# Part of a key sum moved from an accumulator to one-column matmuls, two tiles projected from centred rows, and all engine orders made anew

## Chip, cores, metric

One core of one Trainium2 chip. The metric is device time in microseconds (us), the median over several executions. All runs quoted are of the fast state (a single run is called so); the granted clock in the records is 0.996 to 1.0. Executions of one and the same kernel spread over 0.9 us and more, so an effect of a few tenths is read from traces, not from times.

## The reference, cut

Two layers of linear attention and two gated feed-forward layers, in turn, on a sequence of 2048 rows and width 512 (16 tiles of 128 rows):

```python
phi = lambda t: jnp.where(t > 0, t + 1, jnp.exp(t)) + 1e-6
pq, pk = phi(q), phi(k)                          # q, k, v = layernorm(x) @ wqkv, 32 heads of 16
kv  = jnp.einsum("bhsd,bhse->bhde", pk, v)
z   = jnp.einsum("bhsd->bhd", pk)                # sum of the keys over all rows
num = jnp.einsum("bhqd,bhde->bhqe", pq, kv)
den = jnp.einsum("bhqd,bhd->bhq", pq, z)[..., None] + 1e-6
x = x + (num / den) @ wo                         # layers 0 and 2
x = x + (silu(h @ w_gate) * (h @ w_up)) @ w_down # layers 1 and 3, h = layernorm(x)
```

## The kernel before

Every operation is put on one of five engines in an order that is written out. `PROGRAM` is PE's order; its tokens are a layer digit, a letter and a number. `k4` is the projection of key tile 4, `q23` of the queries of rows group 2, column block 3, `g` the state product pk^T x (four accumulators, 16 tiles), `z` a one-column sum of one tile on PE, `s` the two halves of a sum made elsewhere, `d` denominators, `v`, `m`, `r`, `w` the rest of attention, `u` gate and up, `n` down, `t` a transpose on PE, `S` a spin that keeps PE's clock up. `ORDER` holds the orders of the other engines (`.ts` and `.phi` are DVE's two steps of phi, `.exp` and `.id1` ACT's, `.sq` a sum of squares, `.vpe` variance plus epsilon, `.zs` an addition to the key sum, `.pqn` the scaling of queries by the transposed reciprocal, `.evac` a copy out of an accumulator). `ON_ACT` names what runs on ACT, or on DVE instead of POOL.

```python
def phi(pb, dst, dk, name):
    e = r_e.take()
    on_act = name in ON_ACT
    op("act", lambda a: a.activation(out=etmp[e][:], in_=PB[pb][:], func=ACT.Exp), ...)          # .exp
    if on_act:
        op("act", lambda a: a.activation(out=dst, in_=PB[pb][:], func=ACT.Identity, bias=onep[:]), ...)  # .id1
    op("dve", ... etmp = min(etmp, 1) + 1e-6 ...)                                                # .ts
    if on_act: op("dve", ... dst = max(dst, etmp) ...)               # .phi, two inputs in SBUF
    else:      op("dve", ... dst = max(PB[pb] + 1 + 1e-6, etmp) ...) # .phi, one input in PSUM

def z_add(L, t):                       # layer 2: all 16 tiles, into a float tile zs
    eng = "dve" if f"{L}b{t}" in ON_ACT else "pool"
    op(eng, lambda v: v.tensor_tensor(out=zs, in0=zs, in1=pk[t][:], op=ALU.add), ...)   # .zs

def z_sum(L):                          # token 2s
    op("dve", ... hi = bf16(zs) ...)   # .zh
    op("dve", ... lo = zs - hi ...)    # .zl
    for i, src in enumerate((hi, lo)): # 8 one-column matmuls
        for c in range(NC): mm(pb, src[:, c*P:(c+1)*P], ones[:], ...)
    z_fin(L, pb)                       # mask, on DVE: Zm
# ... cut: layer 0 has a token 0z<t> for each tile (z_acc), 4 one-column matmuls each
# PROGRAM, layer 2:
# 2q20 2q22 2k13 2q23 2g2 2k12 2g7 2g6 2g14 2q13 2s 2d01 2g12 2d02 2g1
# DVE at 49 us:  0q22.phi 0q23.ts 0d0.pqn2 0q23.phi 0G1.evac
```

Of the kernel before, what the change touches and what calls it, by code (L numbers as in the profile page):

```python
# [164 lines left out]

PROGRAM = """
S S S S S S S S S S S S S S S S S S S S S S S S S S S S S S S S S S S S S S S S S S 0t0 S S S S S S S S 0k0 S S S S
0t1 S S S 0t2 S S S 0k1 0k2 S 0t3 0g0 0g1 0k3 0g2 0k4 0k5 0g3 0k10 0g4 0k9 0g5 0k6 0k7 0q03 0z0 0g10 0z4 0k8 0k15
0g7 0k13 0k12 0g9 0k11 0z2 0z10 0z9 0q11 0z3 0z5 0z8 0z15 0g6 0z13 0k14 0q02 0z7 0q10 0q01 0q00 0z1 0g11 0q12 0q21
0z14 0z12 0z6 0z11 0q13 0d02 0d03 0d01 0d00 0g8 0q20 0d11 0q22 0g13 0d12 0d13 0d10 0q23 0d20 0g15 0g12 0g14 0d23  # L170
0d22 0d21 0q30 0v 0q31 0m0 0m1 0m2 0m3 0r2 0w3 0w2 0q33 0w1 0w0 0w5 0w11 0q32 0w7 0w6 0w9 0d33 0w8 0w4 0w10 1u011
1u007 1u005 1u008 1u002 1u006 0d31 0d32 1u012 1u003 1u013 0d30 1u010 1u004 1u000 1u110 1u001 1u009 1n3 0w14 1n0 0w12
1u106 1n1 1u102 1n2 1u107 1u204 0w13 1u101 0w15 1u111 2k2 1u109 1u105 1u103 1u104 1u108 2k0 1u100 2k1 2q00 1u112
1u113 2k3 1n7 1u209 1n6 1u211 1u205 1n4 1n5 1u213 1u200 1u303 1u202 1u203 2q10 1u301 1u208 1u309 1u304 1u206 1u212
2g0 1u201 1u311 1u302 2q11 1u305 1u207 1u310 2q01 1u308 2q03 1u312 2q02 1u210 1n11 1u313 2k4 1u300 1n8 1n10 1u306
1n9 1u307 2k8 1n14 2k7 2k10 2k5 2q21 1n15 2k6 2k9 2k11 1n13 1n12 2q12 2k15 2k14 2g3 2g5 2q20 2q22 2k13 2q23 2g2 2k12
2g7 2g6 2g14 2q13 2s 2d01 2g12 2d02 2g1 2d00 2d03 2d20 2d13 2d21 2q30 2d22 2d10 2d12 2d11 2g13 2q31 2g10 2d23 2g15
2g4 2g9 2g11 2g8 2r1 2q32 2v 2q33 2m0 2m1 2m2 2m3 2d31 2d30 2w0 2w1 2w2 2d32 2w3 2w6 2w5 2w11 2d33 2w4 2w8 2w7 2w9
2w10 3u008 3u000 3u009 3u013 3u010 3u004 3u003 3u005 3u007 3u103 3u110 3u108 3u012 3u002 3u001 3u006 3u104 2w13
3u011 3n3 3u100 2w12 3n2 3n0 3u106 3u105 2w14 3u107 3u111 3n1 3u102 3u109 3u112 3u101 3u113 3n6 3n4 3n5 3n7 3u200  # L180
3u201 3u202 3u203 3u204 2w15 3u205 3u206 3u207 3u208 3u209 3u210 3u211 3u212 3u213 3n8 3n9 3n10 3n11 3u300 3u301
3u302 3u303 3u304 3u305 3u306 3u308 3u307 3u309 3u310 3u311 3u312 3u313 3n12 3n13 3n14 3n15
# [4 lines left out]
i.ld i.ld1 0x2.stats 0x2.sq 0x7.stats 0k0.exp 0t1.xT 0t2.xT 0x10.stats 0k1.exp 0x10.sq 0k2.exp 0t3.xT 0x15.stats  # L187
0x12.stats 0x7.sq 0k3.exp 0x15.sq 0x12.sq 0k4.exp 0k5.exp 0x13.stats 0x13.sq 0k10.exp 0k10.id1 0k9.exp 0k9.id1
0x14.stats 0x14.sq 0k6.exp 0k7.exp 0k6.id1 0q03.exp 0x11.apply 0k8.id1 0k8.exp 0k15.exp 0k15.id1 0k13.exp 0k12.exp
0k13.id1 i.c 0k11.exp 0q11.id1 i.c1 0q11.exp 0k14.id1 0k14.exp 0q02.exp 0q02.id1 0q10.exp 0q01.id1 0q01.exp 0q00.exp  # L190
i.c3 0q12.id1 0q12.exp i.c2 0q21.exp 0q21.id1 0q13.id1 0q13.exp 0d0.rep 0d0.rep2 0q20.exp 0d0.rep1 0q22.exp 0d0.rep3
0q23.exp 0q23.id1 0d1.rep1 0G0.evac 0G2.evac 0G3.evac 0d1.rep 0q30.id1 0q30.exp 0q31.exp 0q31.id1 0M1.evac 0M3.evac
0d1.rep3 0d1.rep2 1x3.sq 1x2.sq 0q33.id1 1x1.sq 0q33.exp 1x0.sq 0q32.exp 1x5.sq 0q32.id1 1x11.sq 1x7.sq 1u011.tanh
1u007.tanh 1x6.sq 1u005.tanh 1u008.tanh 1u002.tanh 1u006.tanh 1x6.apply 1x9.sq 1u012.tanh 1u003.tanh 1u013.tanh
1x4.sq 1u010.tanh 1u004.tanh 1u000.tanh 1x10.sq 0d3.rep2 1u110.tanh 1u001.tanh 0d3.rep 1u009.tanh 1x8.sq 1x10.apply
1x8.apply 1x14.sq 2x3.sq 0d3.rep1 0d3.rep3 2x1.sq 1u102.tanh 1u106.tanh 1u107.tanh 2x2.sq 1u204.tanh 1u101.tanh
2x0.sq 1x13.sq 2k2.id1 1u111.tanh 2k2.exp 1u109.tanh 1u105.tanh 1u103.tanh 2x1.apply 1u104.tanh 1u108.tanh 1x12.sq
2k0.exp 2k0.id1 2k1.id1 2q00.id1 2k1.exp 1u100.tanh 1u112.tanh 1u113.tanh 2q00.exp 1x15.sq 2k3.id1 2k3.exp 2x7.sq
1u209.tanh 2x6.sq 1u211.tanh 1x13.apply 2x4.sq 1u205.tanh 2x6.apply 1u213.tanh 2x5.sq 2x7.apply 1u200.tanh
1u303.tanh 2x5.apply 1u203.tanh 1u202.tanh 2q10.id1 2q10.exp 1u301.tanh 1u208.tanh 1u309.tanh 1u304.tanh 1u206.tanh  # L200
1u212.tanh 1u201.tanh 1u311.tanh 1u302.tanh 2q11.id1 2q11.exp 1u305.tanh 1u207.tanh 1u310.tanh 2q01.exp 2q01.id1
1u308.tanh 2q03.exp 2q03.id1 1u312.tanh 2q02.exp 2q02.id1 1u210.tanh 1u313.tanh 2k4.exp 1u300.tanh 2x11.sq 2k4.id1
2x8.sq 1u306.tanh 2x10.sq 2x8.apply 1u307.tanh 2x9.sq 2x10.apply 2x9.apply 2k8.id1 2k8.exp 2k7.exp 2x14.sq 2k7.id1
2k10.exp 2q21.id1 2k5.id1 2k5.exp 2q21.exp 2k6.exp 2x14.apply 2k9.exp 2x15.sq 2k11.exp 2k9.id1 2x13.sq 2q12.exp
2k15.exp 2x12.sq 2k15.id1 2k14.exp 2q20.exp 2k13.exp 2q22.exp 2q23.id1 2q22.id1 2k12.exp 2q23.exp 2q13.id1 2q13.exp
2d0.rep 2d0.rep1 2d0.rep2 2q31.exp 2q30.exp 2d0.rep3 2q31.id1 2d2.rep 2G0.evac 2G2.evac 2G3.evac 2q32.id1 2d2.rep1
2q32.exp 2d2.rep2 2M0.evac 2M1.evac 2M2.evac 2q33.exp 2q33.id1 2d2.rep3 3x0.sq 3x2.sq 3x1.sq 3x3.sq 3x6.sq 3x5.sq
3x11.sq 3u008.tanh 3u000.tanh 3u009.tanh 3x7.sq 3u013.tanh 3u010.tanh 3x4.sq 3u004.tanh 3u003.tanh 3u005.tanh
2d3.rep 3u103.tanh 2d3.rep1 3u007.tanh 3x9.sq 3u110.tanh 3x8.sq 3u108.tanh 2d3.rep2 3u002.tanh 3u012.tanh 3u001.tanh
2d3.rep3 3u006.tanh 3u104.tanh 3u011.tanh 3u100.tanh 3x13.sq 3x12.sq 3u106.tanh 3u105.tanh 3u107.tanh 3u111.tanh  # L210
3x10.sq 3x13.apply 3u109.tanh 3x10.apply 3u102.tanh 3u101.tanh 3u113.tanh 3u112.tanh 3u200.tanh 3u201.tanh
3u202.tanh 3u203.tanh 3u205.tanh 3u204.tanh 3u207.tanh 3u206.tanh 3u208.tanh 3u209.tanh 3x15.sq 3x14.sq 3u211.tanh
3u210.tanh 3u212.tanh 3u213.tanh 3u300.tanh 3u301.tanh 3u302.tanh 3u303.tanh 3u304.tanh 3u306.tanh 3u305.tanh
3u307.tanh 3u308.tanh 3u309.tanh 3u310.tanh 3u312.tanh 3u311.tanh 3u313.tanh
""",
    "dve": """
i.c 0x0.stats 0x0.aggr 0x0.vpe 0x1.stats 0x1.aggr 0x0.apply 0x3.stats 0t0.xT 0x4.stats 0x3.aggr 0x4.aggr 0x1.apply
0x2.apply 0x5.stats 0k0.ts 0x4.apply 0x5.aggr 0k0.phi 0x3.apply 0x9.stats 0k1.ts 0k1.phi 0x9.aggr 0k2.ts 0x5.apply
0k2.phi 0x6.stats 0x10.apply 0x6.aggr 0x9.apply 0x8.stats 0k3.ts 0k3.phi 0x7.vpe 0x6.apply 0x8.aggr 0k4.ts 0k4.phi
0x7.apply 0k5.ts 0k5.phi 0x12.vpe 0x8.apply 0k10.ts 0k10.phi 0x11.stats 0x11.aggr 0x15.apply 0x11.vpe 0x13.apply  # L220
0x12.apply 0x14.vpe 0k7.ts 0k6.ts 0k7.phi 0q03.ts 0k9.ts 0k9.phi 0k6.phi 0q03.phi 0x14.apply 0k8.ts 0k12.ts 0k15.ts
0k8.phi 0k15.phi 0k12.phi 0k13.ts 0k11.ts 0k13.phi 0k11.phi 0k14.ts 0q11.ts 0q02.ts 0k14.phi 0q11.phi 0q02.phi
0q10.ts 0q10.phi 0q01.ts 0q01.phi 0q00.ts 0q00.phi 0z.zm 0q12.ts 0d0.den 0d0.den1 0q13.ts 0q12.phi 0q13.phi 0q21.ts
0q21.phi 0q20.ts 0q20.phi 0d1.den 0q22.ts 0d1.den1 0q22.phi 0q23.ts 0d0.pqn2 0q23.phi 0G1.evac 0d0.pqn1 0d2.den
0d2.den1 0d0.pqn3 0v.mask 0q30.ts 0d2.den2 0d1.pqn1 0M0.evac 0M2.evac 0d0.pqn 0r2.pqn 0w3.res 0r2.pqn1 0w2.res
0r2.pqn2 1x3.apply 0r2.pqn3 0w1.res 1x2.apply 0w0.res 0d1.pqn3 0d1.pqn2 0q33.ts 1x1.apply 0q33.phi 0d1.pqn 0w5.res
1x0.apply 0w11.res 0w9.res 1x5.vpe 0w7.res 0w6.res 0q32.ts 1x5.apply 0w4.res 1x11.vpe 0w10.res 1x7.vpe 1u011.gst
0w8.res 1u011.h 0q31.ts 1x11.apply 0q31.phi 0q30.phi 1u007.gst 1u007.h 1x6.vpe 1u005.gst 1u008.gst 1u008.h 1u005.h
0q32.phi 1u006.gst 1u006.h 1u002.gst 1u002.h 1u012.gst 1x7.apply 1u012.h 1u003.gst 1x4.vpe 0d3.den 1x4.apply 1u003.h
1x9.apply 1u013.gst 0d3.den1 1u013.h 1u010.gst 1u010.h 1u004.gst 1u004.h 1u000.gst 1u000.h 1u001.gst 1u001.h  # L230
1u009.gst 1u009.h 1u110.gst 0d3.pqn 0d3.pqn2 0w14.res 1u110.h 1n3.res 0d3.pqn3 1n1.res 1u102.gst 1n0.res 0w12.res
# [57 lines left out]
""",  # L289
}  # L290


PE_T = set("""
0d2 0t0 0t1 0t2 0t3 2d1 2z
""".split())
# [13 lines left out]
def bass_interleave_layers__linear_attn_block__swiglu_ffn__prompt_kernel(  # L309
# [20 lines left out]
    with stack:  # L330
# [144 lines left out]
        def ln(L, t):  # L475
# [3 lines left out]
            if (L, g) not in slot_of:  # L479
                slot_of[L, g] = r_xt.take(NF if L % 2 else 2 * TG)  # L480
# [75 lines left out]
        def xt_keys(L, g):  # L556
            return [f"xt{slot_of[L, g]}_{i}" for i in range(TG)]
# [84 lines left out]
        def z_acc(L, t):  # L642
            if L not in zb:
                zb[L] = [bank(pin=True), 0]
# [280 lines left out]
```

## Time and profile before

| | before |
|---|---|
| time, median of 3 | 429.98 us (429.4 to 430.33) |
| span of the profiled run | 428.1 us |
| busy PE / DVE / ACT / POOL | 98 / 67 / 47 / 19 % |
| PE time lost (start to start, less each matmul's pace) | 8.5 us (every gap counted; the prediction's own count gave 7.5), of which 1.50 before `0d23`, 1.08 at `2s`/`2d01`, 0.75 before `0k4`, 0.75 before `3u008` |

With PE busy at 98% the time is PE's work plus the places where PE stands; `0k4` starts at 15.69 us, and at 51 us PE stands behind a late transpose. Five places of the timeline of the kernel before, which are looked at again afterwards. Columns of the timeline: start, length in us, engine, line, operation, output and inputs, form; in brackets the idle time before it and what ended it.

```profile
11.54 0.58 ACT L564 ACTIVATE etmp<-pb 128x512 bf16<-128x512 f32 x1
...
15.69 1.68 PE L409 MATMUL pb<-Wqkv,xnT 128*128 128x512 bf16 x7 [0.58 <-DMA xnT<-xnA]
...
38.84 0.54 POOL L440 DMA_DIRECT2D Wu<-in_B_w_up_dram  x1 [0.49 <-DMA Wu<-in_B_w_up_dram]
...
41.83 0.37 POOL L430 TENSOR_SCALAR_AFFINE_SELECT mask<-mask 128x128 bf16<-128x128 bf16 x1
...
42.56 0.56 PE L409 MATMUL pb<-Zm,pq 128*128 128x8 bf16 x16
...
51.06 0.43 DVE L732 TENSOR_TENSOR pq<-pq,RT 128x512 bf16<-128x512 bf16 x1 [1.83 <-DMA RT<-rrep]
51.88 0.46 PE L409 MATMUL pb<-Zm,pq 128*128 128x8 bf16 x12 [1.33 <-DVE pq L573]
...
239.40 3.82 POOL L626 TENSOR_TENSOR GT<-GT,pk 128x512 f32<-128x512 f32 x3
239.47 1.23 DVE L522 TENSOR_SCALAR xnA<-X,mv,rstd 128x512 bf16<-128x512 bf16 x1
```

`0k4` starts at 15.69 us; the mask's last step on POOL ends at 42.20, DVE's Zm had waited for it, and PE's denominators follow at 42.56, 0.22 us later than its pace allows; at 51 us PE stands behind a late transpose; and at 239.47 a DVE operation that elsewhere takes 0.41 us takes 1.23, while POOL adds to the key sum. The three additions in POOL's line at 239.40 are those of tiles 11, 15 and 14, one behind the other; the second ends at 241.92.

### The profile page before, as it was taken

What the parts mean: (1) busy time and instruction counts of PE and PEld (TensorE: products, weight loads), DVE (VectorE), ACT (ScalarE), POOL (GpSimd) and SP (SyncE); (2) the same over time, 40 slices, a digit from 0 to 9 for tenths busy, and PEclk for the clock granted to TensorE, in tenths of its full rate; (3) what the DMA queues carried; (4) which work ended last, traced back from release to release, by engine and by line L of the source; (5) the groups of instructions that cost most, each with busy time, mean ns of one, the idle gap of its engine ahead of it and who ended that gap; (6) DMA issues with size and microseconds to landing.
All of it is one profiled execution on the core that took longest, in us unless ns stands there. A gap on an engine that the chain in (4) does not pass through costs nothing.

```text
span 428.1 us, 6340 instructions
## 1 busy us (share of the span) xinstructions
PE 419.4 (98%) x2219; PEld 195.5 (46%) x2219; DVE 287.8 (67%) x629; ACT 202.9 (47%) x399; POOL 83.0 (19%) x205
## 2 busy tenths in 40 slices
PE   8999899999999999999999999999999999999997
PEld 6444444444444444444444444344444444444443
DVE  6865799793675476875447869888837606853662
ACT  5998785563356264254465648445312302402220
POOL 5634035210120150001334500431002000100000
PEclk9999999999999999999999999999999999999999
DMA  8639534522011021000021113322110010021001
GB/s 277 141 75 329 126 64 101 146 50 51 4 22 37 2 52 34 2 0 2 2 48 26 25 26 63 62 46 41 38 38 0 13 51 25 0 63 37 2 0 50
DMA packets 53279, 23.21 MB, mean 54 GB/s; under 512 B 46528, under 2 KB 52160, under 8 KB 53248
## 3 DMA queue, kind: packets, MB, share of 16 engines
q1 hardware_dynamic: 51408, 16.27, 17.6%
q0 software_dynamic: 1296, 6.03, 4.1%
q10 hardware_dynamic: 544, 0.52, 0.4%
q8 instruction: 17, 0.28, 0.3%
q14 instruction: 14, 0.11, 0.1%
HBM read 9.70 MB, written 2.10 MB: 28 GB/s over the span
## 4 chain that ended last, share of the span: by engine, by line
PE 88%; DMA 5%; ACT 3%; DVE 2%; issue 1%; SPq 0%; POOL 0%; ACTq 0%; DVEq 0%
PE pb L409 88%; DMA RT<-rrep 2%; DMA xnT<-xnA 1%; DMA X<-in_A_x_dram 1%; ACT pq L567 1%; ACT etmp L564 1%; ACT rrep L719 0%; DVE pq L573 0%; ACT GT L657 0%; DVE pq L732 0%; SPq L723 0%; ACT xnA L498 0%; SPq L440 0%; DVE xnA L522 0%; ACT xnA L495 0%
## 5 line engine op out<-in xcount | busy, mean ns | idle before, releaser
L782 ACT ACTIVATE tht<-pb 128x512 f32<-128x512 f32 x112 | 65.4, 595 | 129.4 <-PE pb L409 106.8
L409 PE MATMUL pb<-xnT,Wg 128*128 128x512 bf16 x448 | 115.0, 379 | 0.6 <-issue 0.6
L409 PE MATMUL pb<-xnT,Wu 128*128 128x512 bf16 x448 | 115.0, 379 | 0.0
L784 DVE SCALAR_TENSOR_TENSOR tht<-tht,pb 128x512 f32<-128x512 f32 x112 | 75.4, 684 | 55.6 <-ACT tht L782 48.9
L409 PE MATMUL pb<-Wd,hT 128*128 128x512 bf16 (+2 forms) x462 | 99.8, 373 | 0.0
L787 DVE TENSOR_TENSOR hT<-tht,pb 128x512 bf16<-128x512 f32 x112 | 74.2, 682 | 2.8
L409 PEld LDWEIGHTS pb<-Wd,hT 128*128 128x128 bf16 x462 | 44.7, 98 | 52.3 <-DVE hT L787 0.2
L409 PEld LDWEIGHTS pb<-xnT,Wu 128*128 128x128 bf16 x448 | 43.6, 98 | 53.1 <-DVE hT L787 0.8
L409 PEld LDWEIGHTS pb<-xnT,Wg 128*128 128x128 bf16 x448 | 43.5, 98 | 53.3 <-issue 1.3
L511 POOL TENSOR_TENSOR rstd<-vpe,negh 128x1 f32<-128x1 f32 x64 | 37.4, 587 | 90.4 <-DVE vpe L507 88.3
L564 ACT ACTIVATE etmp<-pb 128x512 bf16<-128x512 f32 x64 | 37.2, 594 | 21.8 <-PE pb L409 13.1
L501 POOL TENSOR_SCALAR mv<-sums 128x1 f32<-128x1 f32 x55 | 12.8, 239 | 119.8 <-DVE X L810 62.1
L409 PE MATMUL pb<-Wqkv,xnT 128*128 128x512 bf16 x128 | 31.2, 379 | 1.2 <-DMA xnT<-xnA 0.6
L409 PE MATMUL pb<-xnT,Wqkv 128*128 128x512 bf16 x128 | 32.1, 379 | 0.0
L409 PE MATMUL pb<-pk,xnA 128*128 128x512 bf16 x128 | 31.2, 379 | 0.0
L409 PE MATMUL pb<-GT,pq 128*128 128x512 bf16 x128 | 30.2, 379 | 0.2
L498 ACT ACTIVATE xnB<-X,sums 128x512 bf16<-128x512 bf16 x32 | 22.9, 717 | 15.7 <-DVE X L762 8.8
L569 DVE TENSOR_SCALAR etmp<-etmp 128x512 bf16<-128x512 bf16 x64 | 18.7, 304 | 12.1 <-ACT etmp L564 12.0
L762 DVE SCALAR_TENSOR_TENSOR X<-pb,X 128x512 bf16<-128x512 f32 x32 | 21.6, 686 | 7.1 <-PE pb L409 7.0
L810 DVE SCALAR_TENSOR_TENSOR X<-pb,X 128x512 bf16<-128x512 f32 x16 | 11.0, 689 | 19.1 <-PE pb L409 19.0
L498 ACT ACTIVATE xnA<-X,sums 128x512 bf16<-128x512 bf16 x23 | 16.5, 717 | 12.1 <-DVE X L810 11.9
L810 DVE SCALAR_TENSOR_TENSOR pq<-pb,X 128x512 bf16<-128x512 f32 (+2 forms) x17 | 10.9, 656 | 14.4 <-PE pb L409 14.3
(77 smaller groups left out, 309.9 us busy)
## 6 DMA issues: line engine op xcount, KB each, us to landing
out_dram<-pq SPq DMA_DIRECT2D x15, 128.0 KB, 1.8
Wg<-in_B_w_gate_dram POOLq DMA_DIRECT2D x4, 448.0 KB, 4.9
Wu<-in_B_w_up_dram POOLq DMA_DIRECT2D x4, 448.0 KB, 4.6
X<-in_A_x_dram SPq DMA_DIRECT2D x6, 256.0 KB, 4.8
Wd<-in_B_w_down_dram POOLq DMA_DIRECT2D x3, 512.0 KB, 4.7
Wqkv<-in_A_wqkv_dram SPq DMA_DIRECT2D x2, 512.0 KB, 7.0
Wqkv<-in_A_wqkv_dram ACTq DMA_DIRECT2D x2, 256.0 KB, 3.5
X<-in_A_x_dram SPq DMA_DIRECT2D x4, 128.0 KB, 3.4
```

Source lines behind the costliest of these rows:

```text
L409: return op("pe", lambda e: e.matmul(o_ap, lhsT=lhsT, rhs=rhs, start=start, stop=stop, skip_group_check=skip), r=r, w=w, n=n)
L498: op("act", lambda a: a.activation(out=b_ap, in_=X[:, t, :], func=ACT.Square, scale=-float(D), bias=sums[:, t:t + 1], accum_out=mv[:, t, 1 ...
L501: op("pool", lambda p: p.tensor_scalar(out=mv[:, t, 0:1], in0=sums[:, t:t + 1], scalar1=-1.0 / D, scalar2=None, op0=ALU.mult), r=[f"sm{t}" ...
L511: op("pool", lambda p: p.tensor_tensor(out=rstd[:, t:t + 1], in0=vpe[:, t:t + 1], in1=negh[:], op=ALU.pow), r=[f"vp{t}", "negh"], w=[f"rs{ ...
L564: op("act", lambda a: a.activation(out=etmp[e][:], in_=PB[pb][:], func=ACT.Exp), r=[f"pb{pb}"], w=[f"e{e}"], kind="exp")
L567: op("act", lambda a: a.activation(out=dst, in_=PB[pb][:], func=ACT.Identity, bias=onep[:]), r=[f"pb{pb}", "onep"], w=dk, kind="id1")
L569: op("dve", lambda v: v.tensor_scalar(out=etmp[e][:], in0=etmp[e][:], scalar1=1.0, scalar2=1e-6, op0=ALU.min, op1=ALU.add), r=[f"e{e}"], w ...
L762: op("dve", lambda v: v.scalar_tensor_tensor(out=X[:, t, :], in0=PB[pb][:], scalar=1.0, in1=X[:, t, :], op0=ALU.mult, op1=ALU.add, accum_o ...
L782: op("act", lambda e: e.activation(out=tht[a][:], in_=PB[pg][:], func=ACT.Tanh, scale=0.5), r=[f"pb{pg}"], w=[f"th{a}"], kind="tanh")
L784: op("dve", lambda v: v.scalar_tensor_tensor(out=tht[a][:], in0=tht[a][:], scalar=1.0, in1=PB[pg][:], op0=ALU.add, op1=ALU.mult), r=[f"pb{ ...
L787: op("dve", lambda v: v.tensor_tensor(out=hT[h][:, j, :], in0=tht[a][:], in1=PB[pu][:], op=ALU.mult), r=[f"pb{pu}", f"th{a}"], w=[f"h{h}_{ ...
L810: op("dve", lambda v, pb=pb, lo=lo, hi=hi: v.scalar_tensor_tensor(out=o_ap[:, lo:hi], in0=PB[pb][:, 0:hi - lo], scalar=0.5, in1=X[:, t, lo ...
```

## The change

Intent: (1) take the two waits at the end of z in layer 2 away: 13 tiles are summed as before and their halves go to PE early; tiles 12, 13 and 14 get four one-column matmuls each, later. (2) Start earlier: key tiles 0 and 1 of layer 0 are only centred, transposed on PE and projected, and 1/std comes in as the activation's scale. With both, all orders and assignments were made anew: 28 names of `ON_ACT` differ in layers 1 to 3 alone.

```diff
+    if f"{L}c{t}" in PE_T:                                  # centred rows
+        op("dve", ... pq[3][:, t, :] = X[:, t, :] - mean ..., kind="ctr")
+def xt_c(L, t):  # 4 transposes on PE of pq[3], copied to pq[2] by ACT or DVE
-def phi(pb, dst, dk, name):
+def phi(pb, dst, dk, name, by=1.0, rk=()):
-    on_act = name in ON_ACT
+    on_act = name in ON_ACT or bool(rk)
-       ... func=ACT.Exp)
+       ... func=ACT.Exp, scale=by)                          # by = rstd[:, t:t+1] for tiles 0, 1
-       ... func=ACT.Identity, bias=onep[:])
+       ... func=ACT.Identity, bias=onep[:], scale=by)
-    if f"{L}z" in PE_T: z_add(L, t)
+    if t in z_sums[L]:  z_add(L, t)                          # tiles without a token of their own
 # PROGRAM, layer 2
-2q20 2q22 2k13 2q23 2g2 2k12 2g7 2g6 2g14 2q13 2s 2d01 2g12 2d02 2g1
+2q20 2q22 2k13 2z14 2s 2q23 2g2 2k12 2g7 2z13 2g6 2g14 2q13 2z12 2g12 2d01 2d02 2g1
 # PROGRAM, start: 42 spins, then 0t0 ... -> 27 spins, then 0c0 ...   (61 spins in all -> 45)
 # DVE at 49 us
-0q22.phi 0q23.ts 0d0.pqn2 0q23.phi 0G1.evac
+0q22.phi 0d0.pqn 0q23.phi 0G3.evac 0d2.den 0d0.pqn2
 # ... cut: all four orders and ON_ACT made anew
```

## The prediction

> **What bounds the kernel now.** I read the page first: which engine is busy, then the chain that ended last.
>
> ```profile
> span 428.1 us, 6340 instructions
> ...
> PE 419.4 (98%) x2219; PEld 195.5 (46%) x2219; DVE 287.8 (67%) x629; ACT 202.9 (47%) x399; POOL 83.0 (19%) x205
> ...
> PE 88%; DMA 5%; ACT 3%; DVE 2%; issue 1%; SPq 0%; POOL 0%; ACTq 0%; DVEq 0%
> ```
>
> PE is busy 98% of the span and carries 88% of the chain; no other engine is above 67%. So only two things can move the time: PE's amount of work, and the few places where PE stands still. The view of who waited for whom, for PE after the first 16 us, lists those places:
>
> ```profile
> PE pb L409 <- DVE pq L573: 1.3, 1, 1.3
> PE pb L409 <- issue: 0.6, 1, 0.6
> ...
> PE pb L409 <- DVE GT L633: 0.4, 1, 0.4
> PE pb L409 <- DVE Zm L614: 0.4, 1, 0.4
> ```
>
> The lines count gaps after a matmul's modelled end, so they understate. I also took PE's start-to-start distances from the trace and subtracted each matmul's pace (0.215 us for 512 columns, 0.025 us for the one- and eight-column ones, both read from unbroken rows of the trace). That gives about 7.5 us of lost PE time: 4.1 before 15.69 us, 1.5 at 50 to 52 us, 1.07 at 248 to 249 us (the z of layer 2), 0.75 at 276 us, and small change. The change aims at the first and third of these.
>
> The z of layer 2, in order of time, from the timeline (PE, then DVE):
>
> ```profile
> 247.18 1.03 PE L409 MATMUL pb<-xnT,Wqkv 128*128 128x512 bf16 x4
> 248.05 0.24 PE L409 MATMUL pb<-ones,GT 128*128 128x1 bf16 x4
> 248.70 0.25 PE L409 MATMUL pb<-ones,GT 128*128 128x1 bf16 x4 [0.41 <-DVE GT L633]
> 249.34 0.24 PE L409 MATMUL pb<-Zm,pq 128*128 128x8 bf16 x4 [0.39 <-DVE Zm L614]
> ...
> 246.76 0.69 DVE L626 TENSOR_TENSOR GT<-GT,pk 128x512 f32<-128x512 f32 x1
> 247.49 0.43 DVE L632 CAST GT<-GT 128x512 bf16<-128x512 f32 x1
> 247.95 0.69 DVE L633 TENSOR_TENSOR GT<-GT 128x512 bf16<-128x512 f32 x1
> 248.99 0.21 DVE L614 TENSOR_TENSOR Zm<-pb,mask 128x32 bf16<-128x32 f32 x1 [0.35 <-PE pb L409]
> ```
>
> All 16 key tiles are summed in a float accumulator; the last add, the two halves and the mask run one behind the other, and PE meets their ends twice.
>
> Two other places are not what they seem:
>
> ```profile
> 9.80 5.84 DMA xnT<-xnA
> ...
> 46.51 4.53 DMA RT<-rrep
> ```
>
> These are pieces of the chain: two DMA transposes, 5.84 and 4.53 us, where the undisturbed ones of this trace land 2.4 to 2.5 us after their issue. In the trace's landing records 15 of the 16 engines had finished the first at 14.13 us and the last only at 15.64; of the second at 48.93 and 51.03. In the same moments the instruction queue moved one 16 KB packet (at 13.48 us for 1.12, at 49.02 for 0.94). The page's queue list has them:
>
> ```profile
> q8 instruction: 17, 0.28, 0.3%
> ```
>
> 17 packets of 16 KB are PE's instructions: 2219 matmuls, 2219 weight loads and 98 waits are 4536, over 17 is 267 each.
>
> **What the Trainium skill says.** "Runtime: NRT & Kernel Launch", section Instruction fetch mechanics: instructions are refilled in blocks of 16 KiB, 256 instructions, over a DMA queue of the sequencer's own. The 267 agrees. "DMA: Bandwidth & Descriptors", section Queues, rings and completion order: a DMA's semaphore increment lands only after every earlier write of that engine, across its queues. That agrees with one late engine of sixteen: the engine that carries the block. "TensorE: Matmul & The Clock Gate", section Wait — 56ns, not 53.3ns?: 215.7 ns start to start at 512 columns, and not below about 25 ns for small ones; the trace has 0.215 us and 25 ns (20 eight-column matmuls in about 0.5 us). The same page, section What's actually happening: PE runs at half clock until about 3.4 us of activity. The trace shows it: the first spins are 107 ns apart until about 5.2 us and then 55 ns.
>
> **The change, part by part.**
>
> *z of layer 2.* 13 tiles are summed, tiles 12 to 14 go to PE: 12 more one-column matmuls, 12 x 0.025 = +0.30 us. The halves of the sum are now wanted right after the projection of keys 13 (241.13 to 242.0 us). Key 15, the last one summed, was projected at 235.96, so its values are ready near 238.7, its add (1.2 us on POOL) near 240.4 and both halves (0.43 and 0.69 us) near 241.7: before PE asks. Tile 12 (projected at 243.72, ready near 246.9) is wanted behind q13, at about 248.4: ready. The mask (0.21 us) then lies beside the 0.86 us of a product that now stands between z and the denominators. So both waits go: 1.07 - 0.30 = **-0.77 us**.
>
> *Start.* Two tiles are only centred, transposed on PE and projected; 1/std is applied by the activation as its scale, since a key tile has its rows on partitions. The path from statistics to transpose loses vpe, power and scaling: in the trace aggr ends at 4.22 and PE starts at 5.71; centring takes 0.38 us, so PE can start at about 4.7 us, **1.0 us earlier**. The spins fall from 61 to 45, the PE transposes stay at 16. But what counts is when PE gets to key tile 4, at 15.69 us before. Ahead of it lie the same k0 to k3 and g0 to g2. I laid out the new orders of DVE and ACT with the durations of this trace (statistics 0.69, exp 0.60, identity 0.68, square 0.72 us and so on). ACT now does two more identities and puts the second centred copy behind the square of tile 4; k1's exp falls at 11.6 instead of 10.35, g0 can start near 12.6 instead of 11.28, and g2 ends near 15.2 instead of 14.94. Two more DMA transposes (tiles 0 and 1, for the queries) go in the queue ahead of tiles 4 and 5, some 0.6 us of data each behind the weights that end at 13.74: tile 4 lands near 14.8, tile 5 near 15.6. So key tile 4 starts near 15.2 to 15.7: **-0.3 us**, most of the 1.0 us being eaten on ACT and DVE.
>
> *Instruction fetches move.* 16 fewer spins are 32 fewer PE instructions, so through layers 0 and 1 each block is fetched 16 matmuls later in the work (up to 3.4 us). The first then falls not on tile 4's transpose but on one of the next, where keys had 0.7 to 1.6 us of slack.
>
> *The order of DVE at 49 us.* Before, the scaling by the late transpose stood ahead of the last step of q23, and PE waited for q23: 1.5 us. In the changed order the only scaling ahead of q23 is that of the first transpose (landed at 47.63). q23 is then ready near 49.9, PE asks at 50.4, and the next bound is the copying of the four accumulators: **-1.3 us**.
>
> *Other fetches.* The one at 94.41 us no longer meets a transpose that PE waits for: -0.2. Fetches of layer 2 fall nearly as before (4 matmuls later), so the 0.75 us at 276 stay. New collisions elsewhere: +0.5, an estimate from four in this trace that cost 0.2 to 1.5 each.
>
> Sum: -0.3 - 0.77 - 1.3 - 0.2 + 0.5 = **-2.1 us**, so 429.98 - 2.1 = 427.9.
>
> **Rivals.** (1) The start gets worse: the two transposes ahead of tiles 4 and 5 are paced at 1.3 us each in the steady part of the trace; if they cost that much behind the weights, tile 5 lands near 17.5 to 18, and key tile 5 stalls by 1.5 us. For it: the pace; against it: the queue fills while the weights still move. Time then 429.5. (2) The 49 us wait comes back, because the moved fetch hits the first transpose or the copy of the accumulators takes its place: only the z gain and the start remain, 429.0. (3) A clean start: the fetches meet nothing that PE needs and the full 1.0 us of the start survives: 426.5. (4) The early clock: a shorter row of spins with a hole before the first transposes delays full speed by another 3.4 us. The first projection would then take 1.7 us instead of 0.86, but it waits for ACT anyway; 0 to +0.5.
>
> **Range and chances.** One such wait is worth 0.2 to 1.5 us, and three or four of them decide; the three runs of before spread over 0.9 us. Eight in ten: 426.2 to 429.8. 2% is 8.6 us, more than all PE time lost in the kernel (7.5), so faster by over 2% needs all of it: 1%. Slower by 2% would need several new stalls at once: 1%. Within 2%: 98%.
>
> **What would show it.** Right: in PE's waits the two of the z (on the halves and on Zm) are gone and 20 one-column matmuls stand in layer 2 without a gap; the first PE transpose starts near 4.7 us; key tile 4 starts between 15.0 and 15.8 us; no wait of PE on DVE of 1.3 us near 50 us; instruction packets come about 3 us later in the first 120 us. Wrong: key tile 5 waits over 1 us for its DMA transpose, DVE or ACT hold up g0 to g2 past 15.7 us, the wait near 50 us is there again, or a new wait on a late transpose stands in layers 1 to 3.

## The result, and the profile after

| | before, same rounds | after |
|---|---|---|
| median of 4 fast runs | 429.69 us (429.4 to 430.33) | 431.38 us (430.69 to 432.09) |
| ratio, 95% interval | | 1.0038 (1.0016 to 1.0059) |
| span of the profiled run | 428.1 | 429.7 |
| PE time lost | 8.5 us | 11.0 us |

A ratio is the mean time of one kernel's fast runs over that of the other's of the same rounds, so it is not quite the ratio of the medians. Within 2% it is "the same", as predicted at 98%; but the kernel became 1.7 us slower where 2.1 us faster was predicted, and 431.38 lies above the range. From the page after, the busy line and the chain:

```profile
PE 419.6 (98%) x2215; PEld 194.2 (45%) x2215; DVE 288.2 (67%) x625; ACT 207.4 (48%) x402; POOL 83.7 (19%) x210
...
PE 77%; DMA 8%; DVE 7%; ACT 5%; issue 2%; POOL 0%; SPq 0%; POOLq 0%; DVEq 0%; ACTq 0%
```

PE's work is the same (419.4 before), but it carries 77% of the chain and no longer 88%: the rest is steps on DMA, DVE and ACT that PE waited for. Where they came is read by taking the start of the same piece of PE's program in both traces:

| from - to | PE's shift in this stretch, us | predicted |
|---|---|---|
| start to `0k4` | +0.25 | -0.3 |
| to `0d00` (42 us) | +0.62 | 0 |
| to `0d23` (50 us) | -1.48 | -1.3 |
| to `1u011` | -0.05 | |
| to `1u013` (81 us) | +0.60 | |
| to `1n14` | +0.03 | -0.2 (fetch at 94 us) |
| to `2d02`: z of layer 2 | +1.13 | -0.77 |
| to `3u008` | +0.06 | |
| to `3u006` (300 us) | +0.72 | |
| sum | +1.88 | -2.1, with +0.5 for new collisions |

The timeline after at these places, PE, ACT, DVE and POOL:

```profile
4.62 0.59 PE L565 MATMUL pb<-ident,pq 128*128 128x128 bf16 x4 [0.32 <-POOL vpe L511]
...
12.05 0.68 ACT L584 ACTIVATE etmp<-pb,rstd 128x512 bf16<-128x512 f32 x1
12.62 0.78 ACT L587 ACTIVATE pk<-pb,onep,rstd 128x512 bf16<-128x512 f32 x1
13.28 0.60 ACT L584 ACTIVATE etmp<-pb 128x512 bf16<-128x512 f32 x1
...
14.32 0.69 DVE L596 SCALAR_TENSOR_TENSOR pk<-pb,etmp 128x512 bf16<-128x512 f32 x1
15.94 1.24 PE L409 MATMUL pb<-Wqkv,xnT 128*128 128x512 bf16 x5
...
39.95 0.54 POOL L440 DMA_DIRECT2D Wu<-in_B_w_up_dram  x1 [1.77 <-DMA Wu<-in_B_w_up_dram]
...
42.76 0.36 POOL L430 TENSOR_SCALAR_AFFINE_SELECT mask<-mask 128x128 bf16<-128x128 bf16 x1
43.41 0.59 PE L409 MATMUL pb<-Zm,pq 128*128 128x8 bf16 x16 [0.67 <-DVE Zm L642]
...
50.34 0.42 DVE L762 TENSOR_TENSOR pq<-pq,RT 128x512 bf16<-128x512 bf16 x1
51.27 0.45 PE L409 MATMUL pb<-Zm,pq 128*128 128x8 bf16 x12
...
80.39 0.15 DVE L511 TENSOR_SCALAR vpe<-mv 128x1 f32<-128x1 f32 x1 [0.83 <-ACT xnB L498]
81.90 1.02 PE L409 MATMUL pb<-xnT,Wu 128*128 128x512 bf16 x4 [0.44 <-DVE tht L814]
...
235.34 1.15 POOL L654 TENSOR_TENSOR GT<-GT,pk 128x512 f32<-128x512 f32 x1
235.41 1.36 DVE L593 TENSOR_TENSOR pk<-pk,etmp 128x512 bf16<-128x512 bf16 x1 [0.86 <-ACT pk L587]
...
240.74 1.15 POOL L654 TENSOR_TENSOR GT<-GT,pk 128x512 f32<-128x512 f32 x1 [0.17 <-DVE pk L596]
241.41 1.02 PE L409 MATMUL pb<-xnT,Wqkv 128*128 128x512 bf16 x4 [0.62 <-DVE pq L596]
242.29 0.68 DVE L596 SCALAR_TENSOR_TENSOR pk<-pb,etmp 128x512 bf16<-128x512 f32 x1
242.89 0.41 DVE L675 CAST GT<-GT 128x512 bf16<-128x512 f32 x1
243.34 0.69 DVE L676 TENSOR_TENSOR GT<-GT 128x512 bf16<-128x512 f32 x1
244.09 0.25 PE L409 MATMUL pb<-ones,GT 128*128 128x1 bf16 x4 [0.47 <-DVE GT L676]
...
300.57 0.43 DVE L762 TENSOR_TENSOR pq<-pq,RT 128x512 bf16<-128x512 bf16 x1 [1.67 <-DMA RT<-rrep]
```

What to see in it:

- **Start.** PE transposes at 4.62, an early start as foreseen. But ACT works without a gap from 8.39 to 13.88 us, where `k2`'s exp ends; DVE finishes `k2` at 15.01, `g2` begins at 15.06 and `0k4`, behind it, at 15.94.
- **42 us.** POOL's queue issues nine weight loads, one behind the other, and the mask's last step stands behind them. One of them waited 1.77 us for an earlier load (0.49 at the same place before), so the mask is 0.93 us later and PE waits for Zm.
- **50 us.** The scaling by the late transpose is no longer ahead of `q23`; PE's wait is gone.
- **81 us.** The small `vpe` of tile 9 is now on DVE, ahead of an operation that frees an accumulator. It waits 0.83 us for ACT's square, and PE waits for DVE.
- **235 to 244 us.** DVE is held at 235.41 by an identity that ACT did late, then again by POOL's addition; everything behind is late, the bank for `2q22` too. POOL's addition of tile 15 ends at 241.90; DVE is then busy with the steps of tile 14 until 242.97, and the second half of the sum ends at 244.03 and not at the 241.7 of the prediction. The wait on the halves is not gone: it is in another place.
- **300 us.** A reciprocal's transpose, issued at 295.87, lands at 300.54; an instruction block was fetched at 297.7.

### The profile page after: what moved, and what is told of

Same layout as the page of the kernel before. It is cut to its first block, busy times and chain, and to the rows that moved or that the text cites. A ratio compares the mean times of both kernels' runs of the same rounds, so it can differ in the third digit from the quotient of the medians.

```text
span 429.7 us, 6329 instructions
## 1 busy us (share of the span) xinstructions
PE 419.6 (98%) x2215; PEld 194.2 (45%) x2215; DVE 288.2 (67%) x625; ACT 207.4 (48%) x402; POOL 83.7 (19%) x210
## 4 chain that ended last, share of the span: by engine, by line
PE 77%; DMA 8%; DVE 7%; ACT 5%; issue 2%; POOL 0%; SPq 0%; POOLq 0%; DVEq 0%; ACTq 0%
PE pb L409 77%; DMA xnT<-xnB 2%; DMA RT<-rrep 2%; DVE etmp L589 1%; DMA Wu<-in_B_w_up_dram 1%; ACT etmp L584 1%; DMA Wo<-in_A_wo_dram 1%; DMA X<-in_A_x_dram 1%; DVE pk L593 1%; ACT xnA L498 1%; DVE pk L596 1%; ACT pk L587 1%; DMA xnT<-xnA 1%; ACT rrep L749 0%; DVE X L840 0%
## 5 line engine op out<-in xcount | busy, mean ns | idle before, releaser
L584 ACT ACTIVATE etmp<-pb 128x512 bf16<-128x512 f32 x62 | 36.1, 598 | 23.7 <-PE pb L409 14.5
L589 DVE TENSOR_SCALAR etmp<-etmp 128x512 bf16<-128x512 bf16 x64 | 20.2, 327 | 16.9 <-ACT etmp L584 16.6
L498 ACT ACTIVATE xnB<-X,sums 128x512 bf16<-128x512 bf16 x32 | 22.9, 716 | 14.5 <-DMA xnT<-xnB 11.0
L409 PE MATMUL pb<-Wqkv,xnT 128*128 128x512 bf16 x120 | 29.5, 379 | 0.2 <-ACT xnT L554 0.2
L792 DVE SCALAR_TENSOR_TENSOR X<-pb,X 128x512 bf16<-128x512 f32 x32 | 21.4, 684 | 5.5 <-PE pb L409 5.4
L498 ACT ACTIVATE xnA<-X,sums 128x512 bf16<-128x512 bf16 x21 | 15.1, 718 | 15.4 <-DVE X L840 15.1
L840 DVE SCALAR_TENSOR_TENSOR pq<-pb,X 128x512 bf16<-128x512 f32 (+2 forms) x17 | 10.9, 656 | 15.8 <-PE pb L409 13.5
```

What stands on the lines that cost most here:

```text
L409: return op("pe", lambda e: e.matmul(o_ap, lhsT=lhsT, rhs=rhs, start=start, stop=stop, skip_group_check=skip), r=r, w=w, n=n)
L498: op("act", lambda a: a.activation(out=b_ap, in_=X[:, t, :], func=ACT.Square, scale=-float(D), bias=sums[:, t:t + 1], accum_out=mv[:, t, 1 ...
L589: op("dve", lambda v: v.tensor_scalar(out=etmp[e][:], in0=etmp[e][:], scalar1=1.0, scalar2=1e-6, op0=ALU.min, op1=ALU.add), r=[f"e{e}"], w ...
L792: op("dve", lambda v: v.scalar_tensor_tensor(out=X[:, t, :], in0=PB[pb][:], scalar=1.0, in1=X[:, t, :], op0=ALU.mult, op1=ALU.add, accum_o ...
L840: op("dve", lambda v, pb=pb, lo=lo, hi=hi: v.scalar_tensor_tensor(out=o_ap[:, lo:hi], in0=PB[pb][:, 0:hi - lo], scalar=0.5, in1=X[:, t, lo ...
```

## The experiments

### The changed kernel again, and its halves

> The changed kernel once more, unaltered, one look: is the loss made in the same places each time? Theory (in-order waits on DVE and ACT made by the new orders): PE loses time at the same tokens as in its first profile, within 0.1 us each: about 0.8 us before the first denominators of layer 0 (42 us), 0.6 in 1u003 (81 us), 0.8 before 2q22 (240 us), 0.7 inside the sum of layer 2 (243 us), 0.7 in 3u002 (300 us); time 430.7 to 432.1. Rival (chance: instruction fetches fall differently from run to run): two or more of these five are gone or moved, and others have come.

Measured: 431.15 us, one run. The losses are at the same tokens: 1.20 at 42 us, 0.53 at 81, 0.79 and 0.61 in layer 2, but only 0.30 at 300 us. So the losses belong to the kernel; those that hang on the moment of an instruction fetch vary (its first was at 17.0 us in the one run, at 19.8 in this).

Then layer 0 of the change with layers 1 to 3 of the kernel before, and the other way round:

```diff
# start_half
 layer 0:       PROGRAM, ORDER, ON_ACT as after
-layers 1 to 3: as after
+layers 1 to 3: as before (z of layer 2 whole in the accumulator)
# later_half
-layer 0:       as after
+layer 0:       as before
 layers 1 to 3: as after
```

> Layer 0 of the changed kernel (two centred key tiles, 45 spins, its orders), layers 1 to 3 of the kernel before. Theory: the start itself costs +0.25 us, the late mask at 42 us +0.6, the place at 50 us gives -1.5, all else as before: 429.0, ratio to before 0.998 to 1.000. Rival (the start is where the changed kernel loses its 1.7 us): 431, ratio 1.003 or more.

Measured: 430.83 us (429.26 to 432.23), ratio 1.0024 (0.9995 to 1.0054). Up to 269 us it is as expected: PE 0.15 us late at `0k4`, 1.05 lost at 42 us, 1.48 won at 50 us, and 0.45 us ahead through layers 1 and 2. Then a wait of 1.6 us that neither kernel has (timeline, PE):

```profile
271.23 1.04 PE L407 MATMUL pb<-GT,pq 128*128 128x512 bf16 x4 [1.45 <-DVE pq L760]
```

A fetch at 268.3 us falls beside the last reciprocal transpose of layer 2, which lands 4.37 us after its issue (2.4 to 2.5 undisturbed). The profiled run was 0.75 us late at the end because of it. So in the profiled run the expected 429.0 was missed by a collision. spins45 below, which has the same layers 1 to 3 and as few spins, shows it too (1.42 us at the same row; the kernel before loses 0.31 there): which transpose is hit is moved by a change far ahead of it.

> Layer 0 of the kernel before, layers 1 to 3 of the changed one (three tiles of z on PE, its orders and its division of work between engines). Theory: the loss sits here: +0.6 at 81 us (1u003), +1.1 in layer 2 up to the denominators, +0.2 to 0.7 later: 431.5 to 432, ratio 1.004 to 1.006. Rival (the start is at fault): 429 or less, ratio under 1.000.

Measured: 431.3 us (431.02 to 432.05), ratio 1.0039 (1.0019 to 1.0059). Layer 2 costs +1.15 us (`1n14` -0.04, `2d02` +1.11), as in the whole change (+1.13). The losses at 81 and 300 us are absent. At 81 us the small `vpe` is on DVE here too, but PE is 0.8 us later, so that DVE waits 0.28 us for ACT's square and not 0.83, and PE loses 0.05: that loss needs both the moved `vpe` and the time won at 50 us. So most of the slowdown is in layer 2 and has nothing to do with the start.

### The wait at 50 us

```diff
 # q23_first: before, DVE
-0q23.ts 0d0.pqn2 0q23.phi 0G1.evac
+0q23.ts 0q23.phi 0d0.pqn2 0G1.evac
```

> The kernel before with one DVE instruction moved: the scaling of queries by the second transpose of layer 0 (0d0.pqn2) goes behind the last step of q23 instead of ahead of it. Theory: the transpose is still late by some 2 us (an instruction block is fetched beside it), but PE no longer waits for it at 50 to 52 us: that wait falls from 1.5 us to under 0.2, and the time by 1.3 to 1.5 us, to 428.3. Rival (the wait only moves to the copying of the accumulators and the product behind it): under 0.5 us.

Measured: 429.65 against 429.77 us, ratio 0.9997 (0.9976 to 1.0017). The wait at `0d23` is gone (-1.50), but `0v` now waits 0.96 us in pieces for the four accumulator copies, which lie behind other work on DVE and ACT. Net -0.57 from `0d00` to `1u011`, nearer to the rival than to the theory. The start of the profiled run was besides 1 us late, with tile 2 of the input landing at 6.19 and not at 5.50 us. So the copies have to move as well:

```diff
 # q23_evac: before, with
-DVE  0q23.ts 0d0.pqn2 0q23.phi 0G1.evac          +0q23.ts 0q23.phi 0G1.evac 0d0.pqn2
-ACT  0d1.rep1 0G0.evac 0G2.evac 0G3.evac         +0G0.evac 0G2.evac 0G3.evac 0d1.rep1
-POOL nine weight loads, then mask's last step    +mask's last step first
```

> The kernel before with the moved scaling of q23_first, and besides: on DVE the copy of accumulator 1 ahead of that scaling, on ACT one replication (0d1.rep1) behind the three copies of accumulators, on POOL the last mask step ahead of the weight loads. Theory: in q23_first 0.8 us of the 1.35 gained at q23 were lost again just behind it, since the copies waited on ACT and DVE for the late transpose all the same; with these moves that wait stays under 0.3, and the 42 us wait at 0.2 or less: -1.2 us and more, 428.6. Rival: the product behind the copies waits for something else, and the gain stays under 0.6.

Measured: 428.94 against 429.46 us, ratio 0.9985 (0.9971 to 1.0). Both waits are gone, -1.37 us from `0d00` to `0v`; then 0.73 is lost in a wait for the masked state (below; 0.18 in the kernel before), and 0.58 in the rows after it, where copies stand on DVE behind a scaling that waits for its transpose (0.33 before, at another place):

```profile
54.69 1.02 PE L408 MATMUL pb<-Wo,KVT 128*128 128x512 bf16 x4 [0.56 <-DVE KVT L668]
```

From `0d00` to `1u011` -0.6 stays. The changed kernel keeps all of its 1.48 us; it re-made the whole stretch, copies, masked state and second transposes included. Which of these it needs was not tested.

### The start: fewer spins alone

```diff
 # spins45: before, PROGRAM
-42 spins, 0t0 ...
+26 spins, 0t0 ...        # 45 in all, as in the change
```

> The kernel before with 16 of the first 42 spins taken out and nothing else. Theory (the fetch of PE's instructions moves with the count of instructions, and what it meets decides waits): the first block is fetched at 16 to 20 us instead of 13.5 to 14.5; the DMA transpose of tile 4 then lands near 14.2 instead of 15.6 and key tile 4 starts 0.6 to 0.8 us earlier; the third weight load of the gated layer, beside the block fetched near 36.5, is about 1 us late, the last mask step on POOL with it, and PE waits 0.8 to 1.2 us instead of 0.2 before the first denominators (42 us). Sum about 0: 429.5 to 430.3. Rivals: the 42 us wait belongs to the centred start or to the moved mask steps on POOL (then it stays 0.2 here); fewer spins leave PE's clock low[...] (then the first keys come later by 0.5 us or more).

Measured: 431.69 against 429.46 us, ratio 1.0039 (1.0019 to 1.006): a miss. The parts about the fetch held: the first block came at 20.5 us and no longer beside tile 4's transpose, and the mask at 42 us was late by the same chain of weight loads (PE lost 0.97), so that loss comes with fewer PE instructions alone. All traces agree: in the nine traces with 45 spins a block comes at 36.3 to 39.6 us and one load waits 1.7 to 2.1 us for an earlier one; in the five with 61 spins the block comes at 32.8 to 33.7 and no such wait (from the sixth load on) is over 1.0. The second rival came true as well, the clock (timeline, PE):

```profile
8.23 1.86 PE L408 MATMUL pb<-Wqkv,xnT 128*128 128x512 bf16 x4 [1.06 <-DVE xnT L552]
```

1.86 us for what takes 1.02 at full speed: with 16 spins fewer PE stood 1.5 us before its first transposes, and its clock stayed at half until some 12 us. `0k4` came 1.62 us late and the kernel never made it up. The change itself fills this hole with its early transposes, so it does not pay this; the prediction's fourth rival is real, but for another kernel.

### Mending the change

```diff
 # mended: after, with
-POOL i.c5 i.c6, nine weight loads, i.c7 (mask)   +i.c5 i.c6 i.c7, nine weight loads
-DVE  1x9.vpe (before 1u012's operations)          +POOL 1x9.vpe
-ACT  2x13.sq 2k9.id1                              +2k9.id1 2x13.sq
```

> The changed kernel with three small moves, each for one of its waits. (a) The last mask step on POOL ahead of the weight loads: the wait at 42 us falls from 0.8 to 1.2 us to 0.3 or less. (b) The vpe of tile 9 of layer 1 from DVE to POOL: the wait in 1u003 (81 us) falls from 0.6 to under 0.1. (c) The identity of key tile 9 of layer 2 on ACT ahead of the square of tile 13, which waits for a residual: the DVE wait of 0.86 us at 235.4 goes, PE's wait before 2q22 falls from 0.8 to under 0.2 and the one inside the sum of layer 2 from 0.6 to under 0.3. Together 2 us: 429.3, ratio 0.998 to 1.000 to before. Rival (the waits stand for a shortage of DVE or ACT, not for the order): each wait only turns up again within a few us, and the time stays at 431.

Measured: 429.07 against 429.46 us, ratio 0.9986 (0.9971 to 1.0001). The losses at 42 and 81 us are gone, as expected of each edit: these two causes are shown (that at 81 us with the condition that later_half adds). In layer 2 only 0.78 became 0.63 and the sum still waited 0.61. DVE now stands elsewhere (timeline, DVE):

```profile
235.59 0.69 DVE L651 TENSOR_TENSOR GT<-GT,pk 128x512 f32<-128x512 f32 x1 [1.63 <-POOL GT L651]
```

Its own addition of tile 9 to the sum is listed ahead of the residual step that frees a bank, and it must wait for POOL's addition, since all additions go to one tile. A chance loss lies in this run: 1.05 us at `0k7`, whose transpose met the fetch at 21.4 us.

```diff
 # mended2: mended, and on DVE in layer 2
-2k9.phi 2k9.zs 1n12.res 2q12.ts 2x13.apply 2k15.ts 2x12.vpe 2k15.phi 2q12.phi
+2k9.phi 1n12.res 2q12.ts 2q12.phi 2k9.zs 2x13.apply 2k15.ts 2x12.vpe 2k15.phi
 # best_a: mended2, and the halves later in PROGRAM
-2k13 2z14 2s 2q23 2g2 2k12 2g7
+2k13 2z14 2q23 2g2 2k12 2s 2g7
```

> The run mended, and in layer 2 two more moves on DVE: the add of key tile 9 to the sum (it waits for POOL's add of tile 6: 1.63 us idle at 235.6 in mended) and with it everything behind it no longer stands ahead of the residual of tile 12, and the last step of q12, which frees the accumulator that 2q22 waits for, comes ahead of it. Theory (DVE's order made the wait before 2q22): that wait falls from 0.63 us to under 0.15; the wait inside the sum of layer 2 (0.61) falls by less than 0.4, since its halves follow other DVE work. Time 0.5 to 0.9 us below mended at equal luck with the fetches: 428.4. Rival (DVE lacks the time for the halves at this place at all): the 0.6 us turn up at 2q22 or at the sum as before.

Measured: 429.86 against 429.49 us, ratio 1.0006 (0.9993 to 1.0019). The wait at `2q22` is gone and others take its place: 0.23 at `2k13`, 0.64 at `2z14`, 0.14 + 0.61 at `2s`; from `2k6` to `2d02` +0.87 us. The rival was right: the orders of the waits can be shuffled, DVE is simply behind. Why it is behind was the open question (below). Again 1.43 us were lost to a late transpose at `0k7`.

> The run mended2 with the sum of layer 2 asked for behind 2k12 on PE, some 2 us later than in the change. Theory: both waits of z are gone (0.1 us or less inside the sum and before the denominators), and no wait at 2q22; 0.4 to 0.6 us below mended2: 427.9, ratio 0.996 to before. Rival (as in z_late, the wait comes back at a denominator whose query step is late): 0.5 us there, and 428.4.

Measured: 429.63 (428.43 to 430.76) against 429.49 us, ratio 1.0003 (0.9987 to 1.002). The sum's waits are gone and from `2k6` to `2d02` only +0.16 us is left (+0.87 in mended2): asking twelve matmuls (2.6 us) later gives most of it back. `2z14`'s 0.63 us is not gone, and the chance losses (1.18 at `0k7`, 0.30 at 300 us) are in it. Expected better; a miss, in time at least.

### Why DVE is behind: POOL's additions

In the traces above, short DVE operations are now and then much too long (0.28 us becomes 1.25) while POOL adds to the key sum. I took all of two kinds between 100 and 262 us from five traces (before, after, mended2, z_late, best_b): the `.ts` step, and the `.phi` step with two inputs in SBUF. With no addition beside them they take at most 0.30 us (122 cases) and 0.43 us (103 cases). The 18 that began while an addition had 0.3 us or more to go took just what it had to go plus 0.15 us (`.ts`) or 0.28 us (`.phi`), so 0.45 to 1.38 us; the 13 that began first, with an addition starting under them, took 0.29 at most; three with 0.23 us to go took 0.38. The form with an input in PSUM stays at 0.69. The kernel before pays this too: between 200 and 262 us DVE loses some 2.7 us to it, and some 5.0 us in the changed kernel (these two steps and `.apply` counted). The Trainium skill, "SBUF — State Buffer", section Who interferes with whom, says why: DVE and GpSimd share a pair of ports that one instruction holds to its end, and the later one "fully blocks"; DVE needs it in its two-port modes or with two SBUF inputs. The traces agree. A run tests it:

```diff
 # zs_dve: mended2, with the last two additions on DVE
-POOL 2k11.zs ... 2k15.zs
+DVE  2k9.zs 2k11.zs 2x13.apply 2k15.ts 2x12.vpe 2k15.phi 2k15.zs 2k14.ts
```

> This is mended2 with one thing changed: the two additions to z of layer 2 that lie just before its halves (tiles 11 and 15) run on DVE and not on POOL. In mended2 two DVE operations of 0.28 and 0.41 us took 1.25 and 1.27 us (at 238.84 and 240.99) while POOL added (238.68 to 239.93, 240.96 to 242.11), and PE waited 0.23 for tile 13's keys, 0.64 for the lone sum of tile 14 and 0.61 for the halves. Theory (a POOL addition and a DVE operation of two SBUF tiles hold each other up): moved to DVE the two additions cost 0.69 each, no DVE operation of 0.28 to 0.41 takes over 0.5 us between 237 and 242, the lone sum waits at most 0.15 and the halves at most 0.25 us, and PE's shift between 2k6 and 2d02 is about -0.4 and not +0.87; time about 428.9 (ratio 0.998). Rival (DVE simply has too much to do there, and the length of those two operations is an artefact of the record): DVE gets 1.4 us more work, the halves are as late or later than in mended2 (243.23 end of the second at 243.92), the waits stay at 1.2 us or more in sum, time 429.9 or above.

Measured: 428.61 (428.25 to 428.88) against 429.58 us, ratio 0.9971 (0.9945 to 0.9996). Timeline of mended2, POOL and DVE, at the addition of tile 11:

```profile
238.68 1.25 POOL L651 TENSOR_TENSOR GT<-GT,pk 128x512 f32<-128x512 f32 x1 [1.40 <-DVE GT L651]
238.84 1.25 DVE L586 TENSOR_SCALAR etmp<-etmp 128x512 bf16<-128x512 bf16 x1
```

and of zs_dve, the same DVE step, and PE's next wait:

```profile
237.67 0.29 DVE L586 TENSOR_SCALAR etmp<-etmp 128x512 bf16<-128x512 bf16 x1
...
240.34 1.04 PE L406 MATMUL pb<-Wqkv,xnT 128*128 128x512 bf16 x4 [0.81 <-DMA xnT<-xnA]
```

1.25 us became 0.29, no short DVE step is over 0.5, the wait at `2z14` is gone and that on the halves fell from 0.61 to 0.30. So the mechanism is shown, and the rival's "artefact of the record" falls: DVE did 1.4 us more work and was ready 0.4 us earlier, against PE's start of `2k6`. The size is not what the theory gave: an addition now stands ahead of `2x13.apply`, so tile 13's transpose leaves later and PE waits 0.98 us at `2k13` (0.23 in mended2). From `2k6` to `2d02` it is +0.51 us, where -0.4 was expected and mended2 had +0.87. The larger part of the better time, in the profiled runs, is that this one had no late transpose at `0k7`.

### The idea of z alone, and the best of both

```diff
 # z_late: before, with z of tiles 12 to 14 on PE, the halves and lone sums placed late
-2q23 2g2 2k12 2g7 2g6 2g14 2q13 2s 2d01 2g12 2d02 2g1
+2q23 2g2 2k12 2g7 2z14 2z13 2g6 2g14 2s 2q13 2z12 2g12 2d01 2d02 2g1
-POOL 2k14.zs 2k13.zs      -DVE 2k12.zs; 2s.zh 2s.zl directly behind 2q22.phi
```

> The kernel before with its own layer 0 and its own division of work; of the change only the three tiles of z of layer 2 on PE, and the sum asked for later than in the change (behind 2g14 instead of behind 2k13), the two halves on DVE behind q22. Theory: the idea is sound where the halves have time: both z waits (0.55 and 0.53 us) go, 12 one-column matmuls cost 0.3, so -0.7 to -0.8 us at the denominators, 429.1. Rival (putting the two halves, 1.15 us of DVE, earlier makes k12 or q13 late): a new wait of 0.5 us or more at z12 or at the denominators, and nothing gained.

Measured: 429.26 against 429.46 us, ratio 0.9994 (0.9979 to 1.0009). Both waits of the z are gone and `2d02` comes 0.79 us earlier relative to before, the -0.77 of the prediction. Then `2d13` waits 0.51 us for `q13`, whose step got behind others on DVE.

```diff
 # best_b: layer 0 of the change with the mask's step ahead of the weight loads,
 #         layers 1 to 3 of before with z_late, and on DVE 2q13.phi directly behind 2q13.ts
```

> Layer 0 of the change with the last mask step ahead of the weight loads; layers 1 to 3 of the kernel before with the z of z_late, and the last step of q13 ahead of that of q23 on DVE. Theory: layer 0 is 0.7 to 1.2 us ahead of before at the first gated product (as in mended, unless a fetch meets a key's transpose), the z gives another 0.7 since the 0.5 us wait at 2d13 of z_late goes: 428.0, ratio 0.996. Rival (16 fewer spins move a fetch onto a late replication transpose of layer 2, as in start_half and spins45, 1.4 to 1.6 us at 270 us): 429.3 or more.

Measured: **427.79 us (427.55 to 428.44) against 429.49, ratio 0.9964 (0.9951 to 0.9977)**, the fastest of all and faster than both kernels, by less than 2%. PE is 1.26 us ahead at `1u011`, gains 0.78 at the z and keeps both. The halves stand on PE without a wait (timeline, PE):

```profile
245.89 0.34 PE L407 MATMUL pb<-ones,GT 128*128 128x1 bf16 x8
```

That this is close to the 427.9 of the prediction's sum is in part luck: `0k4` is 0.23 us late and not 0.3 early, and the 0.5 us set aside for new collisions was not lost.

## Why the prediction was wrong, point by point

**Right.** PE's first transposes at 4.62 us (4.7); tile 4 landing at 14.74 and tile 5 at 15.90 (14.8 and 15.6), so the first rival was wrong; the wait before `0d23` gone, -1.48 (-1.3). That the z idea is worth 0.77 us: 0.79 in z_late and 0.78 in best_b, but not in the kernel at hand.

**The step that failed: "So both waits go: 1.07 - 0.30 = -0.77 us".** The halves were said to be ready near 241.7, ahead of PE. They were ready at 244.03, and the stretch gave +1.13 us: 1.9 us off, half of the whole miss of 3.8 to 4.0 us. Term by term: key 15 was to be ready at 238.7 and was at 240.66; its addition was to end at 240.4 and ended at 241.90; the halves were to follow at once and began at 242.89, behind the steps of tile 14 on DVE. The working took each duration from undisturbed rows and left out what stands in each engine's order. Part of it was wrong for the kernel before already: there key 15 is ready at 239.35, and its addition, behind that of tile 11 on POOL, ends at 241.92. With such times the halves are ready at 243.0 at the earliest (241.92 + 0.43 + 0.69), and PE asks right behind key 13, at 242.0; z_late, which asks some 5 us later, gives -0.79.

In the changed kernel came besides an identity put behind a square on ACT (0.86 us of DVE) and the lock between POOL's additions and DVE (three steps of 0.28 to 0.42 us took 1.36, 1.25 and 0.87). mended took the first away and met the next, an addition of DVE waiting for POOL's ahead of a step that frees a bank; mended2 took that away and met the lock, which zs_dve shows. No single one gives back the 1.9 us; the orders of before with the z idea put into them and the later request do. Whether the new order or the new division of work (the 28 names) puts DVE behind was not separated.

**The term "+0.5 for new collisions" was mis-sized.** It measured +0.62 at 42 us and +0.72 at 300 us, both with an instruction block beside the late transfer; +0.60 at 81 us has another cause, a small operation moved from POOL to DVE. The step "The one at 94.41 us no longer meets a transpose that PE waits for: -0.2" failed in the profiled run: the block came at 94.54 and the same transpose landed 3.62 us after issue (3.59 before); in the second run PE did gain 0.23. That blocks come 3 us later held for the first two (17.0 and 36.5 us, 13.5 and 32.8 before), not for the next three. At 50 us the block still hit the second transpose, 4.37 us from issue to landing (4.53 before); the new order took the wait away, as predicted. The 42 us loss could have been foreseen: in the trace of before PE already lost 0.22 us to this mask, which stands behind nine loads, of which the last five each wait for an earlier one. That the fetch delays the loads is shown by spins45 in as far as fewer PE instructions alone bring it; that the mask's place is what makes it cost, by mended and best_b.

**The start, -0.3, gave +0.25** (0.00 to +0.31 at `0k4` in all eight profiled runs with this start). The step "I laid out the new orders of DVE and ACT with the durations of this trace (... exp 0.60, identity 0.68 ...)" put the end of `g2` at 15.2; it was 15.94. Exp and identity of the two centred tiles take a per-row scale, and so 0.68 and 0.78 us (0.60 and 0.69 without it). All four lie in ACT's unbroken chain ahead of `k2`, for which `g2` waits: an estimate of 4 x 0.085 = 0.34 of the 0.74 us. The Trainium skill, "ScalarE: Activation LUTs", section What ACT_TABLE_LOAD costs, has it: each pointer operand of 128 x 1 adds about 93 ns; the trace shows 80 and 89. I had not looked there. No run was made for this alone; the other 0.40 us I did not take apart.

**Open.** In the prediction's two cases of a late transpose only one engine of sixteen was late; in start_half, in spins45 and in the changed kernel at 300 us all sixteen parts came late (the first of them 4.0 to 4.6 us after issue). Why is not known. Nor is it known what sets the moment of a fetch: with the same PE program up to there the first one came between 17.0 and 24.2 us in eight runs; with 61 spins it came between 13.2 and 14.5 in five.

## What to carry to other kernels

When one engine is at 98%, a change is worth what its waits are worth, and a new order of the other engines is a change of its own: put a good idea into the order that works, and move only what it needs. Check for each duration in the sum whether something runs beside it: a POOL addition of 128 x 512 floats that is already running holds back a short DVE step on SBUF (0.28 or 0.42 us) until it ends. And what stands in a queue behind loads (a mask, a constant) has to be put ahead of them if anything else needs it.

## What the Trainium skill lacked or had wrong

- "Runtime: NRT & Kernel Launch", Instruction fetch mechanics, calls the cost of a block boundary "mostly hidden". Here the cost shows in a DMA transpose that meets the block. In the fourteen traces, after 16 us, the 990 transposes with no PE block moving between issue and landing took 2.4 us (median; 941 of them at most 2.64), the 139 with one took 3.6 us (107 of them over 3.0), and PE lost 0.2 to 1.6 us where it waited for one. No page gives this cost.
- No page says that the number of spins or matmuls ahead moves every later fetch, so that a change at the start can cost 1.6 us at 271 us (start_half; 1.4 at 274 us in spins45).
- "SBUF — State Buffer", Who interferes with whom: right, and worth a figure for POOL additions of 128 x 512 floats: a DVE step of 0.28 us took 1.25.
